# The second walk of a second feed-forward: its second product by 2x2 blocks, with weight operands kept in DRAM

## The chip, the cores and the metric

The kernel runs on one core of one Trainium2 chip. The metric is the device time of one execution in microseconds; the number quoted is the median of three runs. Besides the runs there is one profiled execution, whose page and trace are read here. TensorE multiplies matrices into the eight banks of PSUM; VectorE, ScalarE and GpSimd work elementwise, GpSimd on SBUF alone; SyncE (SP) issues all DMAs of this kernel, whose data go through 16 DMA engines. In the profile PE is TensorE, PEld its weight loads, DVE VectorE, ACT ScalarE, POOL GpSimd, SP SyncE.

## The reference, cut

```python
def _attn_ref(q, k, v):                    # 4 batches, 8 heads, 576 positions, 64 features
    scores = scale * np.matmul(q, k.transpose(0, 1, 3, 2))
    scores = np.where(block_i >= block_j, scores, -1e9)      # blocks of 64 positions
    attn = softmax(scores)
    return np.matmul(attn, v)

def _moe_ref(x, w_gate, w_val, w_out, rms_g):       # 2304 tokens, 512 -> 1536 -> 512
    xn = x / rms(x) * rms_g
    g = xn @ w_gate
    return (g * sigmoid(g) * (xn @ w_val)) @ w_out

def _moe2_ref(x, w_gate, w1, w2):                   # 8 experts, 512 -> 1024 -> 512
    logits = x @ w_gate
    P = np.exp(logits - logits.max())
    for _ in range(8):
        P /= P.sum(1, keepdims=True) + 1e-09
        P /= P.sum(0, keepdims=True) + 1e-09
        P *= N / E
    out = 0
    for e in range(E):
        h = np.maximum(x @ w1[e], 0.0)
        out += P[:, e:e + 1] * (h @ w2[e])
    return out
```

The function computes attention, then the first feed-forward on the 2304 x 512 result, then the second. In the second every token goes through all 8 experts, and P weighs what they return.

## The kernel before

**Precision.** Every large product is made from two-part operands: a value is split into a rounded high part (fp32r) and the rest, and a product is three matmuls, high by high, high by low and low by high (`THREE`). The helper `copy` makes the high part (line 294 on ScalarE, line 298 on VectorE), `minus` the low part (line 307, on GpSimd or VectorE). A split is thus one operation of each kind.

**Order.** Nothing is issued where it stands in the code. Each operation goes into `G` (class `Graph`) with an engine, a duration, what it reads and writes and, where two engines could do it, an alternative. A planner then lists all of them, forwards and backwards for twelve rounds, and the order with the earliest planned end is issued on each engine. Durations of type `Both` (two-input operations on GpSimd, and on VectorE where both inputs are in SBUF) exclude each other in the plan. SP's DMAs are ordered by the same plan. Buffers come from rings: the next use of a tile depends on all users of its last one.

**The second feed-forward, `moe2`.** Its input x stays in `acc[0]` to `acc[4]`, features on partitions, in token blocks of 512, 512, 512, 384 and 384 (`BL`). It is walked twice. `PASSES` (line 1028) names the token ranges of each walk: the first takes blocks 0 and 1 as one pair of halves of 512, the second blocks 3 and 4 as halves of 384 and block 2 as halves of 256. In each walk the loop runs over 8 experts and `NG` = 4 groups of two blocks of 128 hidden units; expert and group together are called a step here, 32 in a walk.

- `pass_operands` and `operands` prepare x for a walk: seven combinations of its 2x2 blocks, each split, into the tiles `xs` and, for a second pair of ranges, `more`. A combination of blocks is a subtraction (`add`, line 1064).
- `weights1` loads two raw blocks of w1 (`RAW`, 3 tiles), makes four sums of 256 columns (line 1064) and four split operand tiles (`W`, 9 tiles of [128, 2, 512]). Two w2 tiles come through `L.get` (line 330 for the DMA).
- `up` (line 1219) makes the first product by Strassen's seven products, six matmuls each, in three banks X, Y and Z of the four in `UP`. X takes products 0, 5, 6 and 3, and between them ScalarE keeps its sum (`keep`, line 1228); VectorE adds (`plus`, line 1233), ScalarE and VectorE apply relu and split the result into `HT2` (lines 1239, 1241).
- `down` (line 1275) makes the second product in the plain way: for each tile of 128 tokens, two hidden blocks by three terms, six matmuls of 512 columns into one of the three banks of `DN`. VectorE multiplies by P and adds into `acc`, over x (line 1290; for expert 0 lines 1281 and 1284). At the last step a tile goes to `out` (line 1294).
- `sink` computes P in the first step of the first walk, by a chain on VectorE with small matmuls (line 1177).

Both walks load w1 and w2 and prepare them again. `up` of a step stands ahead of `down` of the step before, and the planner mixes the two.

## Time and profile before

| | us |
|---|---|
| median of three runs | 2270.88 |
| lowest and highest run | 2269.70, 2271.71 |
| span of the profiled execution, first to last instruction | 2269.8 |
| TensorE busy in it | 2225.1 |
| VectorE, ScalarE, GpSimd busy | 1382.3, 986.1, 948.5 |

The profile gives no other time of the profiled execution than its span; it lies within the three runs. Attention and the first feed-forward take about the first 765 us, the first walk of the second feed-forward lasts to about 1415, the second to the end. Busy times are unions of the intervals of an engine's instructions; a matmul's own duration overlaps the next one's, so the time of one matmul is best read from the length of an unbroken row of them, divided by their count. The chain that ended last is followed back from the last instruction to what released it each time.

### The profile page before, as it was taken

The page shows a single profiled execution, that of the slowest core. Times are in us where ns is not written, and L with a number is a line of the kernel's source. Part 1 is how long each engine was busy: PE and PEld are TensorE (multiplying, and loading weights), DVE is VectorE, ACT ScalarE, POOL GpSimd, SP SyncE. Part 2 cuts the span into 40 slices and gives each one's busy share as a digit, 9 for nine tenths or more (in the row PEclk, how much of TensorE's full clock was granted, in tenths as well). Part 3 has the DMA queues.
Part 4 walks back from the last instruction along what each step waited for, and adds up shares of the span by engine and source line. Part 5 has one row for each costly group of instructions (what it writes and reads, how often), then busy time and mean ns, then how long its engine had stood idle before and what let it go on. Part 6 is the DMA issues. An engine that isn't in the chain of part 4 may idle for free.

```text
span 2269.8 us, 30396 instructions
## 1 busy us (share of the span) xinstructions
PE 2225.1 (98%) x11196; PEld 1908.5 (84%) x11196; DVE 1382.3 (61%) x2397; ACT 986.1 (43%) x2138; POOL 948.5 (42%) x899
## 2 busy tenths in 40 slices
PE   8799989999999999999999999999999999999999
PEld 6577778888999978888888888899999999999898
DVE  7879966776632566555555556655555555555555
ACT  6688756575311433333333334533333333333332
POOL 6555732321411544444444446543334443343431
PEclk8899999999999999999999999999999999999999
DMA  7645666443676111111111111211111111111111
GB/s 191 182 138 185 217 212 194 160 164 112 221 254 211 52 51 52 52 51 51 51 56 47 52 51 42 89 42 43 38 38 44 46 38 42 38 39 46 42 42 47
DMA packets 89416, 211.46 MB, mean 93 GB/s; under 512 B 14890, under 2 KB 18218, under 8 KB 89268
## 3 DMA queue, kind: packets, MB, share of 16 engines
q1 hardware_dynamic: 89268, 209.52, 29.7%
q8 instruction: 88, 1.44, 0.3%
q14 instruction: 60, 0.49, 0.1%
HBM read 185.89 MB, written 23.59 MB: 92 GB/s over the span
## 4 chain that ended last, share of the span: by engine, by line
PE 89%; DVE 7%; ACT 2%; issue 1%; POOL 1%; SPq 0%; DMA 0%; DVEq 0%; ACTq 0%; POOLq 0%
PE pm L1275 34%; PE ps L1219 24%; PE pm L913 11%; PE pm L1219 7%; PE pm L944 6%; PE ps L689 2%; PE ps L485 2%; PE po L732 1%; DVE mn L494 1%; PE po L1137 1%; DVE acc L354 1%; DVE acc L356 1%; PE po L599 1%; ACT p L679 0%; DVE ptl L696 0%
## 5 line engine op out<-in xcount | busy, mean ns | idle before, releaser
L1219 PE MATMUL ps<-xs,w 128*128 128x384 f32 (+2 forms) x2640 | 548.5, 350 | 0.0
L1290 DVE SCALAR_TENSOR_TENSOR acc<-pm,Pm,acc 128x512 f32<-128x512 f32 x504 | 378.1, 750 | 266.9 <-PE pm L1275 265.4
L1219 PEld LDWEIGHTS ps<-xs,w 128*128 128x128 f32 x2640 | 467.8, 189 | 51.6 <-issue 0.3
L1275 PE MATMUL pm<-w,h 128*128 128x512 f32 x1920 | 461.5, 390 | 0.0
L307 POOL TENSOR_TENSOR w<-raw,w 128x512 fp32r<-128x512 f32 (+1 forms) x289 | 345.2, 1204 | 173.8 <-ACT w L294 166.2
L1275 PEld LDWEIGHTS pm<-w,h 128*128 128x128 f32 x1920 | 354.1, 188 | 69.7
L307 POOL TENSOR_TENSOR w<-sp,w 128x512 fp32r<-128x512 f32 x126 | 170.0, 1350 | 511.4 <-ACT w L294 511.2
L1275 PE MATMUL pm<-w,x 128*128 128x512 f32 x1536 | 369.2, 391 | 0.0
L1275 PEld LDWEIGHTS pm<-w,x 128*128 128x128 f32 x1536 | 287.2, 188 | 56.9
L913 PE MATMUL pm<-x,w 128*128 128x512 f32 (+1 forms) x1440 | 331.0, 377 | 2.3 <-POOL w L307 1.4
L913 PEld LDWEIGHTS pm<-x,w 128*128 128x128 f32 x1440 | 259.5, 191 | 34.4 <-POOL w L307 2.2
L294 ACT ACTIVATE w<-sp 128x512 fp32r<-128x512 f32 x128 | 80.7, 631 | 292.4 <-PE pm L1275 286.9
L1228 ACT ACTIVATE ct<-ps 128x384 f32<-128x384 f32 (+2 forms) x152 | 75.9, 499 | 236.1 <-PE ps L1219 236.1
L1233 DVE TENSOR_TENSOR ct<-ps,ct 128x512 f32<-128x512 f32 (+2 forms) x154 | 86.2, 561 | 137.3 <-ACT ct L1228 71.3
L944 PE MATMUL pm<-h,w 128*128 128x512 f32 (+1 forms) x720 | 163.9, 374 | 1.2 <-DVE t L928 1.2
L294 ACT ACTIVATE w<-raw 128x512 fp32r<-128x512 f32 (+1 forms) x292 | 162.0, 575 | 6.2 <-PE pm L913 2.8
L1219 PE MATMUL pm<-xs,w 128*128 128x512 f32 (+2 forms) x720 | 155.6, 341 | 0.0
L307 POOL TENSOR_TENSOR h<-t,h 128x512 fp32r<-128x512 f32 (+1 forms) x56 | 67.7, 1209 | 195.8 <-ACT h L294 195.4
L944 PEld LDWEIGHTS pm<-h,w 128*128 128x128 f32 x720 | 129.6, 190 | 17.5 <-DVE t L928 1.6
L1219 PEld LDWEIGHTS pm<-xs,w 128*128 128x128 f32 x720 | 124.2, 188 | 17.4
L1239 ACT ACTIVATE h<-ct 128x384 fp32r<-128x384 f32 (+1 forms) x99 | 55.5, 561 | 89.5 <-DVE ct L1233 89.5
L1064 POOL TENSOR_TENSOR sp<-raw 128x256 f32<-128x256 f32 x64 | 51.5, 804 | 83.5 <-DMA raw<-w_dram 83.5
(268 smaller groups left out, 2892.0 us busy)
## 6 DMA issues: line engine op xcount, KB each, us to landing
raw<-w_dram SPq DMA_DIRECT2D x256, 256.0 KB, 2.6
w<-kg SPq DMA_DIRECT2D x48, 512.0 KB, 4.3
w<-kv SPq DMA_DIRECT2D x48, 512.0 KB, 3.9
w<-ko SPq DMA_DIRECT2D x48, 512.0 KB, 3.9
rq<-qT_dram SPq DMA_DIRECT2D x56, 144.0 KB, 4.2
rq<-kT_dram SPq DMA_DIRECT2D x52, 144.0 KB, 3.6
acc<-wg_dram SPq DMA_DIRECT2D x12, 512.0 KB, 4.2
acc<-wv_dram SPq DMA_DIRECT2D x12, 512.0 KB, 4.3
```

The costliest lines, as they stand in the source:

```text
L294: nc.scalar.activation(out=out_(), in_=in_(), func=AF.Copy, scale=scale)
L307: eng.tensor_tensor(out=out_(), in0=a(), in1=b(), op=ALU.subtract)
L485: nc.tensor.matmul(out=ps()[:, o : o + n], lhsT=a[:, 128 * t : 128 * t + 128], rhs=c[:, k0 : k0 + n], start=start, stop=stop)
L913: nc.tensor.matmul(out=ps()[:, 0:n], lhsT=w()[:, a, 128 * k : 128 * k + 128], rhs=xv()[:, c, k, 0:n], start=k == 0 and (a, c) == (0, 0), s ...
L944: nc.tensor.matmul(out=ps()[:, 0:n], lhsT=wos[q]()[:, a, 128 * m : 128 * m + 128], rhs=ht()[:, c, 0:n], start=q == 0 and (a, c) == (0, 0), ...
L1064: eng.tensor_tensor(out=out_(), in0=a(), in1=b(), op=op)
L1219: nc.tensor.matmul(out=bank()[:, 0:n], lhsT=w()[:, a, o + 128 * k : o + 128 * k + 128], rhs=views[p, q, i, k, c](), start=start and k == 0 ...
L1228: G.op("ACT", t_act(n, True), lambda: nc.scalar.activation(out=t()[:, 0:n], in_=bank()[:, 0:n], func=AF.Copy), r=[bank], w=[t])
L1233: G.op("DVE", t_v1(n), lambda: nc.vector.tensor_tensor(out=t()[:, 0:n], in0=bank()[:, 0:n], in1=t()[:, 0:n], op=ALU.add), r=[bank, t], w=[t])
L1239: G.op("ACT", t_act(n, psum), lambda: nc.scalar.activation(out=ht()[:, 0, 0:n], in_=src()[:, 0:n], func=AF.Relu), r=[src], w=[ht])
L1275: nc.tensor.matmul(out=y(), lhsT=hs[f][half]()[:, a, 128 * t : 128 * t + 128], rhs=ws[f]()[:, c, :], start=f == 0 and (a, c) == (0, 0), st ...
L1290: G.op("DVE", 63 + t_v1(512), lambda y=y, dst=dst, tt=tt, e=e: nc.vector.scalar_tensor_tensor(out=dst(), in0=y(), scalar=Pm()[:, tt, e : e ...
```

## The change

- The token ranges are dealt out anew. The first walk takes 1280 tokens in two groups, of width 384 (blocks 0 and 1) and 256 (the remaining 128 of each, against the first 256 of block 2, in two pieces). The second takes 1024 tokens in one group of width 512 (blocks 3 and 4, and the last 256 of block 2).
- In the first walk `down` is as before. Prepared w1 tiles are written to DRAM as they are (`keep_w`, `first_w`). `weights2` splits the two w2 tiles, makes four sums of them, splits these too into the ring `EX`, and writes what the second walk needs (`second_w`). The first walk's `CT` has 6 tiles in place of 7, and accumulators of block 2 lie in two pieces, so that x of the second walk stays.
- The second walk prepares no weights: `reload` reads seven tiles of 512 KB for the first product of two steps and seven for the second.
- In the second walk relu multiplies by P at once (`scaled`). P is turned in `sink`, written to DRAM and read back spread over the partitions, two DMAs for each half and expert (`load_p`).
- The second product works on a pair of steps, with the result's features on partitions: the two hidden blocks of a step, the two halves of the tokens and the two halves of the 512 features are its 2x2 blocks, and both steps of the pair are summed in the same banks. `sums` and `produce` make seven combinations of h's blocks, each split, in the ring `HL` (10 tiles, 14 used for a pair). `down2` makes seven products, each for two halves of 128 features and with six matmuls a half, in banks X, Y and Z, of which X again takes several products; after every product `gather` adds the bank to one of eight accumulators.
- At the end the accumulators are turned by 32 transposes, evicted, and stored.

The diff, its core:

```diff
-    PASSES = [[((0, 0), (1, 0), 512)], [((3, 0), (4, 0), 384), ((2, 0), (2, 256), 256)]]
+    PASSES = [[[((0, 0), (1, 0), 384)], [((0, 384), (2, 0), 128), ((1, 384), (2, 128), 128)]],
+              [[((3, 0), (4, 0), 384), ((2, 256), (2, 384), 128)]]]
+    WIDTH = [[sum(x[2] for x in q) for q in p] for p in PASSES]
+    LEFT = 10
...
+        def two(t, o, n):
+            return t[:, o : o + 2 * n].rearrange("p (a n) -> p a n", a=2)
+
+        HT2 = ring_of(order4 + [two(xt0, 768 * i, 384) for i in range(4)], [set(b.users) for b in HT[-4:]] + [done4] * 4)
+        pad = late(lambda p: p.tile([128, 4608], F32, name="pad"))
+
+        def cut(o, n):
+            return lambda: pad()[:, o : o + n]
+
+        atts = set(att_ops)
+        CT = ring_of([*T1.tiles, *(cut(3072 + 384 * i, 384) for i in range(4))],
+                     [set().union(*(b.users for b in T1[-2:]))] * 2 + [atts] * 4)
+        SP_ = ring_of([cut(512 * i, 512) for i in range(4)], [atts] * 4)
+        EX = ring_of([two(xt0, 3072, 512), lambda: two(pad().bitcast(F32R), 2048, 512)], [done4, atts])
...
+            pq = PO.next()
+            G.op("PE", 115, lambda: nc.tensor.transpose(
+                out=pq()[0 : (TT - LEFT) * E, 0:128], in_=Pm()[:, LEFT:TT, :].rearrange("p t e -> p (t e)"), identity=ident_t),
+                r=[Pm, ident], w=[pq])
+            G.op("ACT", 250, lambda: nc.scalar.activation(out=pt(), in_=pq()[0 : (TT - LEFT) * E, 0:128], func=AF.Copy), r=[pq], w=[pt])
+            G.op("SP", 300, lambda: nc.sync.dma_start(out=ptd_t.rearrange("t e n -> (t e) n"), in_=pt()), r=[pt], w=[ptd], lat=2000)
...
+        def keep_w(kept_, key, w, cols, g, prio):
+
+            if key not in kept_:
+                t = scr.tile([128, 2, 512], F32, name=f"{'f' if kept_ is first_w else 's'}{'_'.join(map(str, key))}")
+                kept_[key] = fixed(t, par=True)
+            b = kept_[key]
+            o = 0 if cols == 512 else 256 * (g % 2)
+            G.op("SP", 1900 * cols // 512, lambda: nc.sync.dma_start(out=b()[:, :, o : o + cols], in_=f32(w()[:, :, 0:cols])),
+                 r=[w], w=[b], prio=prio + 1, lat=2000)
...
+            for name, src, b, n in (("a", r0, [r0], 512), ("b", lambda: r1()[:, 256:512], [r1], 256), ("c", p0, s[0:2], 512), ("d", p1, s[2:4], 512)):
+                w = parts(src, b, n, W, prio)
+                keep_w(first_w, (name, e, g if n == 512 else g // 2), w, n, g, prio)
                 ws.append(w)
...
+        def weights2(e, g, prio):
+
+            r0, r1 = raws([w2[e, 128 * f : 128 * f + 128, :] for f in (GF * g, GF * g + 1)], prio)
+            ws = [parts(r_, [r_], 512, W, prio) for r_ in (r0, r1)]
+            p0, p1, s = sums4(lambda: r0()[:, 0:256], lambda: r1()[:, 0:256], lambda: r0()[:, 256:512], lambda: r1()[:, 256:512],
+                              (r0, r1, r0, r1), prio)
+            keep_w(second_w, ("a", e, g // 2), ws[0], 256, g, prio)
+            keep_w(second_w, ("b", e, g), ws[1], 512, g, prio)
+            for name, src, b in (("c", p0, s[0:2]), ("d", p1, s[2:4])):
+                keep_w(second_w, (name, e, g), parts(src, b, 512, EX, prio), 512, g, prio)
+            return ws
+
+        def reload(ring, kept_, order, prio):
+            out = {}
+            for key in order:
+                w, b = ring.next(), kept_[key]
+                G.op("SP", 1900, lambda w=w, b=b: nc.sync.dma_start(out=f32(w()), in_=b()), r=[b], w=[w], prio=prio, lat=2000)
+                out[key] = w
+            return out
...
-            h11 = relu(plus(Y, s1))
...
+        accc = [[Buf(place_c(j, t)) for t in range(k)] for j, k in ((0, 4), (1, 4), (2, 2))]
...
+        def second_pass():
+
+            N = WIDTH[1][0]
+            small = ended(CT, SP_, EX)
+            hops = ended(HT2, EX)
+            sides = ended(*more)
+            wbufs = W[-W.n :]
+            WL = ring_of([b.get() for b in wbufs] + [two(xt0, 1024 * i, 512) for i in (0, 1)], [set(b.users) for b in wbufs] + [hops] * 2)
+            HL = ring_of(order4 + [two(xt0, 1024 * i, 512) for i in (2, 3)] + [two(xt1, 1024 * i, 512) for i in range(4)],
+                         [hops] * 6 + [sides] * 4)
+            rb = RAW[-RAW.n :]
+            CF = ring_of([*T1.tiles, *(cut(512 * i, 512) for i in range(9)), rb[0].get()], [small] * 11 + [set(rb[0].users)])
+            xs = pass_operands(1, CF)[0]
+            used = ended(CF) | small | rb[0].users
+            over = [(j, i) for j, k in ((2, 4), (3, 3), (4, 3)) for i in range(k)]
+            CT1 = ring_of([*CF.tiles, *(acc[j][:, 512 * i : 512 * i + 512] for j, i in over)],
+                          [used] * CF.n + [read_x[j, 1] | ended(*accc[j : j + 1]) for j, i in over])
...
+            def scaled(src, half, n, psum=False):
+                t, P = CT1.next() if psum else src, pv_[0][half]
+                G.op("DVE", t_v1(n) if psum else t_vv(n), lambda: nc.vector.scalar_tensor_tensor(
+                    out=t()[:, 0:n], in0=src()[:, 0:n], scalar=0.0, in1=P(), op0=ALU.max, op1=ALU.mult),
+                    r=[src, P], w=[t])
+                return t
...
+            def diff(dst, x, y):
+                add(N, v(dst), v(x), v(y), op=ALU.subtract, r=[x, y], w=[dst], margin=GAIN)
+                return dst
+
+            def sums(h):
+                (b11, b12), (b21, b22) = h
+                got = {0: b11, 1: b21, 2: b22, 6: b12}
+                got[4] = diff(CT1.next(), b12, b11)
+                got[5] = diff(CT1.next(), b22, got[4])
+                return got
+
+            def produce(gots, ops, i):
+                ops[i] = []
+                for got in gots:
+                    if i == 6:
+                        diff(got[6], got[2], got[6])
+                    if i == 3:
+                        got[3] = diff(got[5], got[1], got[5])
+                    x, ht = got[i], HL.next()
+                    copy(G.op, N, lambda ht=ht: ht()[:, 0, 0:N], v(x), r=[x], w=[ht], margin=GAIN)
+                    minus(G.op, N, lambda ht=ht: ht()[:, 1, 0:N], v(x), lambda ht=ht: f32(ht()[:, 0, 0:N]), r=[x, ht], w=[ht], margin=GAIN)
+                    ops[i].append(ht)
...
+            def gather(bank, key):
+                dst = ac[key]
+                if key in begun:
+                    G.op("DVE", t_v1(N), lambda: nc.vector.tensor_tensor(out=dst(), in0=bank()[:, 0:N], in1=dst(), op=ALU.add),
+                         r=[bank, dst], w=[dst])
+                else:
+                    begun.add(key)
+                    G.op("ACT", t_act(N, True), lambda: nc.scalar.activation(out=dst(), in_=bank()[:, 0:N], func=AF.Copy), r=[bank], w=[dst])
...
+            def down2(e, grp, gots, ops):
+                g0, g1 = 2 * grp, 2 * grp + 1
+                ws = reload(WL, second_w, [("a", e, grp), ("b", e, g0), ("b", e, g1), ("c", e, g0), ("c", e, g1), ("d", e, g0), ("d", e, g1)], 0.5)
+                wts = {0: [(ws["a", e, grp], 256 * (g % 2)) for g in (g0, g1)]}
+                for i, name, o in ((1, "b", 0), (3, "b", 256), (4, "c", 0), (5, "c", 256), (6, "d", 0), (2, "d", 256)):
+                    wts[i] = [(ws[name, e, g], o) for g in (g0, g1)]
+
+                def m(i, dt, bank, start):
+                    def go():
+                        for gi in range(2):
+                            w, o = wts[i][gi]
+                            o += 128 * dt
+                            for a, c in THREE:
+                                nc.tensor.matmul(
+                                    out=bank()[:, 0:N], lhsT=w()[:, a, o : o + 128], rhs=ops[i][gi]()[:, c, 0:N],
+                                    start=start and gi == 0 and (a, c) == (0, 0), stop=gi == 1 and (a, c) == (1, 0),
+                                    skip_group_check=not start)
+
+                    G.op("PE", 6 * t_mm(N), go, r=[*(w for w, o in wts[i]), *ops[i]], w=[bank], prio=2.0)
+
+                X, Y, Z = {}, {}, {}
+                for i, B, new, key in ((0, X, True, (0, 0)), (1, Y, True, (0, 0)), (5, X, False, (0, 1)), (4, Z, True, (1, 1)),
+                                       (6, X, False, (1, 1)), (2, Z, False, (0, 1)), (3, X, False, (1, 0))):
+                    if i not in ops:
+                        produce(gots, ops, i)
+                    for dt in range(2):
+                        if new:
+                            B[dt] = (DX if B is X else DY).next()
+                        m(i, dt, B[dt], new)
+                        gather(B[dt], (*key, dt))
...
+            pend = None
+            for e in range(E):
+                load_p(e)
+                for grp in range(NG // 2):
+                    g0, g1 = 2 * grp, 2 * grp + 1
+                    f = reload(WL, first_w, [("a", e, g0), ("c", e, g0), ("d", e, g0), ("b", e, grp), ("a", e, g1), ("c", e, g1), ("d", e, g1)], 0.5)
+                    gots = []
+                    for g in (g0, g1):
+                        wa, wb, wc, wd = f["a", e, g], f["b", e, grp], f["c", e, g], f["d", e, g]
+                        gots.append(sums(up(1, 0, xs, [(wa, 0), (wa, 256), (wd, 256), (wb, 256 * (g % 2)), (wc, 0), (wc, 256), (wd, 0)], CT1, scaled)))
+                    if pend:
+                        down2(*pend)
+                    ops = {}
+                    for i in ORDER[:5]:
+                        produce(gots, ops, i)
+                    pend = (e, grp, gots, ops)
+            down2(*pend)
+            for half in range(2):
+                for t in range(N // 128):
+                    bank, stage = UP.next(), CT1.next()
+                    tt = LEFT + half_tiles[half][t]
+
+                    def turn(half=half, t=t, bank=bank):
+                        for m_ in range(4):
+                            nc.tensor.transpose(out=bank()[:, 128 * m_ : 128 * m_ + 128],
+                                                in_=ac[m_ // 2, half, m_ % 2]()[:, 128 * t : 128 * t + 128], identity=ident_t)
+
+                    G.op("PE", 4 * 115, turn, r=[ident, *(ac[d, half, dt] for d in range(2) for dt in range(2))], w=[bank], prio=2.0)
+                    G.op("ACT", t_act(512, True), lambda bank=bank, stage=stage: nc.scalar.activation(out=stage(), in_=bank(), func=AF.Copy),
+                         r=[bank], w=[stage],
+                         alts=[("DVE", t_v1(512), lambda bank=bank, stage=stage: nc.vector.tensor_copy(out=stage(), in_=bank()))])
+                    G.op("SP", 1100, lambda stage=stage, tt=tt: nc.sync.dma_start(out=out[128 * tt : 128 * tt + 128, :], in_=stage()), r=[stage])
+
+        first_pass()
+        second_pass()
```

## Rows read from the trace of the kernel before

**Rows 1.** the page: span, busy time by engine, GB/s in 40 slices

```profile
span 2269.8 us, 30396 instructions
...
PE 2225.1 (98%) x11196; PEld 1908.5 (84%) x11196; DVE 1382.3 (61%) x2397; ACT 986.1 (43%) x2138; POOL 948.5 (42%) x899
...
GB/s 191 182 138 185 217 212 194 160 164 112 221 254 211 52 51 52 52 51 51 51 56 47 52 51 42 89 42 43 38 38 44 46 38 42 38 39 46 42 42 47
```

**Rows 2.** the windows by stage; the first line names the columns

```profile
core 0: us, PE busy (x) PEld busy (x) DVE busy (x) ACT busy (x) POOL busy (x), PEclk, DMA share, GB/s
...
1500.00:2250.00 750.00, 750.00 (x4142) 678.83 (x4141) 409.95 (x700) 258.60 (x570) 284.15 (x281) 1.00 0.14 39
620.00:670.00 50.00, 50.00 (x290) 50.00 (x290) 17.86 (x33) 8.14 (x16) 8.10 (x8) 1.00 0.76 254
780.00:820.00 40.00, 38.11 (x174) 30.98 (x173) 33.38 (x79) 19.56 (x35) 20.71 (x19) 1.00 0.16 48
1400.00:1440.00 40.00, 40.00 (x194) 34.36 (x194) 34.60 (x49) 20.05 (x46) 28.54 (x30) 1.00 0.23 76
```

**Rows 3.** the chain that ended last, first walk: start us, us, what

```profile
850.12 4.08 PE ps L1219 x18
...
919.92 8.18 PE pm L1275 x36
932.23 4.08 PE ps L1219 x18
```

**Rows 4.** the same chain, second walk, two steps apart

```profile
1530.52 4.18 PE ps L1219 x24
...
1582.70 5.22 PE ps L1219 x30
```

**Rows 5.** groups by shape, 800 to 2270 us: count | busy us, mean ns | idle

```profile
L307 POOL TENSOR_TENSOR w<-raw,w 128x512 fp32r<-128x512 f32 x181 | 237.0, 1324 | 124.6 <-ACT w L294 124.0 <-DMA raw<-w_dram 0.6
...
L294 ACT ACTIVATE w<-raw 128x512 fp32r<-128x512 f32 x183 | 108.3, 623 | 0.0
...
L1064 POOL TENSOR_TENSOR sp<-raw,raw 128x256 f32<-128x256 f32 x61 | 46.7, 765 | 0.0
...
L1284 DVE TENSOR_TENSOR acc<-pm,acc 128x512 f32<-128x512 f32 x54 | 37.3, 691 | 29.8 <-PE pm L1275 29.3
...
L1228 ACT ACTIVATE ct<-ps 128x512 f32<-128x512 f32 x49 | 29.3, 598 | 52.8 <-PE ps L1219 52.7
```

**Rows 6.** timeline of GpSimd in the first walk: start us, us, engine, line

```profile
1010.95 1.29 POOL L307 TENSOR_TENSOR w<-sp,w 128x512 fp32r<-128x512 f32 x1 [4.20 <-ACT w L294]
...
1017.75 1.47 POOL L307 TENSOR_TENSOR w<-raw,w 128x512 fp32r<-128x512 f32 x1
```

**Rows 7.** timeline of VectorE there

```profile
999.95 1.01 DVE L1241 SCALAR_TENSOR_TENSOR x<-t,x 128x512 fp32r<-128x512 f32 x1
...
1005.47 0.68 DVE L1241 SCALAR_TENSOR_TENSOR x<-t,x 128x512 fp32r<-128x512 f32 x1
```

**Rows 8.** DMA issues: KB each, median us from issue to landing

```profile
w<-kg SPq DMA_DIRECT2D x48, 512.0 KB, 4.3
...
kg<-w SPq DMA_DIRECT2D x12, 512.0 KB, 4.3
```

**Rows 9.** groups by shape, TensorE, whole span: the transposes of attention

```profile
L689 PE MATMUL ps<-ident,p 128*128 128x128 f32 x247 | 54.5, 292 | 3.2 <-ACT p L679 1.8 <-ACT p L501 1.3
```

**Rows 10.** the end of the chain, 2240 to 2270 us

```profile
2266.09 0.75 DVE acc L1290
```

**Rows 11.** tile xs, 1395 to 1480 us: count, ns min/median/max, first and last start

```profile
L307 DVE TENSOR_TENSOR xs<-ct,xs x7: 545/959/1368, 1410.0 to 1432.6; 128x384 fp32r<-128x384 f32 x6, 128x256 fp32r<-128x256 f32 x1
...
L307 POOL TENSOR_TENSOR xs<-acc,xs x3: 1013/1057/1193, 1403.6 to 1419.2; 128x384 fp32r<-128x384 f32 x2, 128x256 fp32r<-128x256 f32 x1
```

**Rows 12.** the chain between the walks

```profile
1412.56 8.18 PE pm L1275 x36
```

**Rows 13.** timeline of TensorE early in the first walk; idle before it in brackets

```profile
798.71 0.39 PE L1177 MATMUL po<-sm,onec 128*128 128x8 f32 x2 [1.18 <-DVE sm L1165]
```

269 lines of the change are left out of this document (163 added, 106 removed).

## The prediction

> **What bounds the kernel now.** I read the page first: TensorE is busy for 98% of a span of 2269.8 us [rows 1]. The windows by stage come next, because a mean over attention, first feed-forward and second feed-forward says little about one of them. In the second walk of the second feed-forward (1500 to 2250 us) TensorE is busy for 750.00 of 750 us, VectorE for 410, ScalarE for 259, GpSimd for 284; the granted clock is 1.00, the upper level of 2.4 GHz, and the DMA engines move 39 GB/s [rows 2]. The chain of waits through both walks holds matmuls and nothing else. In the first walk the same place of the pattern returns after 82.11 us, which is four steps of 20.53 us; in the second walk two steps take 52.18 us, or 26.09 each [rows 3, 4]. So this part is worth what its matmuls cost: a matmul taken away is time taken away, as long as the other engines and the transfers stay under it.
>
> One 512-column matmul costs 8.18 / 36 = 0.2272 us [rows 3]. The Trainium skill (TensorE: Matmul & The Clock Gate, "Back-to-back issue gap") gives about 0.2157 us for a warm one; the row is 5% above that, the row decides, and by the page's figure the saving below would be 41.4 us in place of 43.6.
>
> **The matmuls.** A step is one expert and two blocks of 128 hidden units; there are 32 in a walk. Before, the first walk takes 1024 tokens and the second 1280. The change swaps this: the first now takes 1280 in widths 384 and 256 (the old second walk's shapes), the second 1024 in width 512 (the old first walk's). The first product is already Strassen's and keeps its counts at each width, so it costs the same. The second product was (8 + 10) token tiles x 6 matmuls x 32 steps = 3456 of 512 columns. After: 10 x 6 x 32 = 1920 in the first walk, and in the second 16 pairs of steps with 7 products x 2 halves x 2 steps x 3 terms = 84 each, so 1344. That is 192 fewer: 192 x 0.2272 = **-43.6 us**. A pair of steps of the second walk holds 84 + 84 matmuls, 168 x 0.2272 = 38.2 us; a step of the first should stay at 26.1.
>
> **The tail.** The new accumulator has features on partitions, so 8 tiles are turned at the end by 32 transposes of 128x128. The attention's are the nearest row, 54.5 / 247 = 0.22 us each [rows 9]: **+7.0 us**, all after the last product, since nothing else is left for TensorE. Bounds: 3.5 if the half whose sums end first is turned under the last product, 9 if its banks wait for their copies. What follows, one eviction and one store, replaces the 0.75 us addition and the store that end the old chain [rows 10]; I count that as nothing.
>
> **The first walk's added work.** Per step w2 gets four 256-column sums and two more operand pairs, on GpSimd 4 x 0.765 + 2 x 1.324 = 5.7 us, on ScalarE 2 x 0.62 = 1.2 us [rows 5]. The old second walk has 284/750 x 26.09 = 9.9 us of GpSimd and 9.0 of ScalarE in a step [rows 2]; 15.6 and 10.2 stay under 26.1, so the price is nothing. It costs if GpSimd work is late, and the slack against that is 10 us a step. Eight stores join four loads on SP's queue: 3.67 MB out, 1.05 MB in, 181 GB/s. The loads of the next raw weights stand behind those stores on SP; a 512 KB store lands in a median of 4.3 us, a load the same [rows 8], and 254 GB/s have been moved at 620 to 670 us under a TensorE that never paused [rows 2]. Price nothing, with the second rival for the case that this is wrong.
>
> **The second walk's moved work.** The raw loads, sums and splits of the weights go; they were hidden, so nothing is gained. Seven 512 KB loads per product come instead: 14 x 0.524 MB in 38.2 us, 192 GB/s, under the 254 shown [rows 2]. The tiles are asked for half a pair (19 us) or at least half an up-product pair (9.5 us) ahead of use, against 4.3 us to land [rows 8]. New is the work on h: per pair of steps 8 differences and 14 subtractions on GpSimd or VectorE, 14 copies on ScalarE or VectorE, 14 gatherings from PSUM and 14 operations that end the first product on VectorE. At the rows' durations: GpSimd 22 x 1.29 = 28.4 us if it takes all [rows 6]; VectorE 22 from PSUM x 0.691 + 6 from SBUF x 0.68 = 19.3 us [rows 5, 7]; ScalarE 6 x 0.598 + 14 x 0.623 = 12.3 us [rows 5]. All lie under 38.2. The gathering that a bank waits for has three products of other banks, 3 x 1.36 = 4.1 us, to be done in. I take 0.15 us a pair for waits, +2.4 us; bounds 0 and 1.0 a pair.
>
> What speaks against this is that GpSimd and VectorE don't run freely beside each other. VectorE's two-SBUF-input operation takes 0.68 us alone and 1.01 beside GpSimd [rows 7], GpSimd's 1.29 and 1.47 [rows 6]. The Trainium skill (SBUF — State Buffer, "Who interferes with whom") says why: such an operation and one of GpSimd hold the shared pair one at a time, each for a whole instruction. By that rule the two columns add, and the trace's stretched rows agree.
>
> Added, GpSimd's 28.4 and VectorE's six, 4.1, make 32.5 us of 38.2: 85%, still under. Each operation moved from GpSimd to VectorE takes 0.6 us off. With all at their stretched lengths it is 22 x 1.47 + 6 x 1.01 = 38.4, just at TensorE's 38.2. That is the first rival.
>
> **The two transitions.** Into the first walk: TensorE idles 1.9 us in 780 to 820, part of it in the chain of normalising steps (one wait of 1.18 us on VectorE) [rows 2, 13]. The operands now come in three pieces of 384, 128 and 128 columns, three times the instructions for 640 columns in place of 512, and VectorE is busy 33 of 40 us there. I add 1.5, bounds -1.9 and 8. Between the walks: before, all is hidden (40.00 of 40 us busy) [rows 2], since after the last up-product at 1412.56 two full second products are left to do [rows 12]. Now 10 tiles are left, 10 x 1.36 = 13.6 us, and up to four products that need no kept sum, 5.4 us, together 19. Preparing the operands is 44 two-input operations, half of 384 and half of 128 columns. A 384 one takes 0.96 us on VectorE in the median and 0.55 at best, 1.06 on GpSimd [rows 11]; with both engines at it about 0.5 each, and 0.25 for the short ones, 22 x 0.75 = 16.5 us, and VectorE also drains ten banks. The first kept sum waits for the whole preparation, because its ring begins with the same buffers. So it ends 18 to 22 us after the last up-product: 0 to 3 us idle. Then two pairs of up-products run with no second product to fill the time in which a bank is read, some 0.7 us (0.598 [rows 5] and a hand-over) once in each of four. Together **+4 us**, bounds 0 and 10.
>
> **The sum**, on the profiled span: 2269.8 - 43.6 + 7.0 + 2.4 + 1.5 + 4 = 2241.1. The runs' median, 2270.88, is 1.1 above that span: **2242 us**.
>
> **Rivals.** *The shared pair decides the second walk.* The sum at stretched lengths, 38.4 of 38.2, says it is close; a gathering queued behind a blocked VectorE operation then lets a bank wait. Against it: the stretched row is the exception, and the planner treats the pair as exclusive when it orders the work. Price: one GpSimd operation's wait, 1.29 us, per pair, 16 x 1.29 = 21 us: 2263. Chance 0.17.
>
> *The transfers decide (the slower one).* Stores of the first walk at 141 GB/s have no row: before, the whole trace has 36 weight stores, three groups of 12 [rows 8]. If the mix of stores and loads falls below 4.72 MB in 26.98 us, 175 GB/s, each step loses the 0.89 us that is its share of the 28.6 us gained, and the kernel is no faster. At 160 GB/s a step takes 29.5 us: 32 x 3.4 = 109 us, 2351. For it: the slices of the span in which those stores fall moved between 112 and 217 GB/s, though nothing says that they wanted more [rows 1]; against it: 254 under loads [rows 2]. Chance 0.06.
>
> *The up-products aren't filled.* The second walk has two up-products of a step pair in a row. If the order doesn't put second products between them, each loses about 0.7 us where its bank is read, 32 x 0.7 = 22 us: 2264. The old first walk mixes them, and the new one has as many fillers as products. Chance 0.09.
>
> *The change does less than it says*, the saved matmuls given back by an idle TensorE in unforeseen places: 2271. Chance 0.04.
>
> **How the numbers follow.** The forecast has the remaining 0.64. Its own bounds: 2242 less 3.5 (tail), 2.4, 3.4 and 4 is 2229 if all fall together; plus 2, 14, 6.5 and 6 is 2270, as unlikely. The range 2232 to 2264 leaves out the slower cases and the extremes. A measurement of this kernel tells 0.2% from nothing: below 2266.3 all of the forecast but 0.01, and the first and third rival nearly whole, 0.87; between, 0.05; above 2275.4, 0.08.
>
> **What would show it.** After: 11196 - 192 + 33 = 11037 matmuls; first-walk steps of 26.1 us at some 180 GB/s; pairs of 38.2 us in the second walk, VectorE and GpSimd both under 0.9 there; GpSimd busy near 15.6 of 26.1 in a first-walk step; a gap of a few us between the walks; some 7 us more between the last product and the end. A pair of 39.5 us with TensorE waiting for VectorE points to the first rival, a step well over 26 us with waits on DMA to the second, gaps behind ScalarE's evictions to the third. The forecast is wrong if any steady step is not TensorE's.

## The result and the profile after

The changed kernel takes 2245.28 us (median of 4 runs, 2244.82 to 2247.61) against 2270.29 of the kernel before beside it: a ratio of 0.9892, with a 95% interval from 0.9878 to 0.9906. It is faster by 1.1%, 25 us where 29 were forecast. The profiled execution has a span of 2243.6 us, 26.2 less than before.

The page of the changed kernel, the lines that answer to [rows 1]:

```profile
span 2243.6 us, 31476 instructions
...
PE 2196.7 (98%) x11037; PEld 1884.6 (84%) x11037; DVE 1445.1 (64%) x2450; ACT 990.3 (44%) x2140; POOL 1167.4 (52%) x1077
...
HBM read 273.97 MB, written 141.07 MB: 185 GB/s over the span
```

The count of matmuls is the one forecast, 11037, and TensorE's busy time falls by 28.4 us. GpSimd works 219 us more. The windows of the changed kernel by stage (columns: us, then busy time and instructions of each engine, granted clock, DMA share, GB/s), beside [rows 2]: three in which the routing is computed, the first walk, the place between the walks, the second walk.

```profile
755.00:765.00 10.00, 10.00 (x50) 10.00 (x50) 4.30 (x9) 2.90 (x7) 5.82 (x6) 0.66 0.57 211
765.00:775.00 10.00, 10.00 (x43) 10.00 (x43) 3.90 (x8) 2.84 (x10) 4.01 (x8) 0.51 0.08 26
775.00:785.00 10.00, 6.65 (x33) 6.02 (x32) 7.89 (x20) 3.35 (x11) 7.43 (x13) 0.84 0.13 52
830.00:1600.00 770.00, 770.00 (x4256) 697.07 (x4255) 437.59 (x729) 300.64 (x652) 445.96 (x454) 1.00 0.51 179
1600.00:1640.00 40.00, 38.52 (x177) 31.18 (x176) 28.85 (x49) 16.77 (x41) 22.72 (x27) 1.00 0.75 261
1740.00:2180.00 440.00, 439.99 (x1921) 359.44 (x1920) 300.95 (x384) 142.59 (x233) 257.05 (x192) 1.00 0.60 198
```

Both walks are still TensorE's, to the last hundredth in the first and 439.99 of 440 in the second, at the upper clock. In the second walk VectorE is busy for 68% and GpSimd for 58%. What stands out is the start: TensorE counts as busy from 755 to 775 us, at a mean of 0.66 and then 0.51 of its clock, which is in the second of these windows nearly all the time the lower level of 1.2 GHz; then it is idle for a third of 775 to 785.

The chain of waits (start us, us, what) in the first walk, two steps apart, and in the second, at the same place of the pattern three pairs of steps apart; it answers to [rows 3, 4]:

```profile
932.99 5.22 PE ps L1296 x30
...
985.14 5.22 PE ps L1296 x30
...
1739.57 4.08 PE pm L1518 x18
...
1855.33 4.08 PE pm L1518 x18
```

A step of the first walk takes 52.15 / 2 = 26.08 us (26.1 forecast), a pair of the second 115.76 / 3 = 38.59 (38.2, and 0.15 for waits). A part of the 0.4 us above the matmuls is in the walks of before too, whose step of 20.53 us holds 90 matmuls, 90 x 0.2272 = 20.45; the table counts what is added.

Where the 26.2 us come from, by comparing TensorE's start-to-start times in the two traces, stage by stage (the matmuls' row is their count at the row's rate; 0.2 us are not placed):

| | forecast | measured |
|---|---|---|
| 192 matmuls less | -43.6 | -43.6 |
| attention and first feed-forward (same order of matmuls in both) | 0 | -1.6 |
| start of the first walk, with the routing | +1.5 | +8.5 |
| steady first walk | 0 | 0 |
| between the walks | +4 | +2.6 |
| waits in the second walk | +2.4 | +3.6 |
| tail | +7.0 | +4.5 |
| sum | -28.7 | -26.0 |

### The profile page after: what moved, and what is told of

Its sections match the earlier page's. It is cut to its first block, busy times and chain, and to the rows that moved or that the text cites. A ratio compares the mean times of both kernels' runs of the same rounds, so it can differ in the third digit from the quotient of the medians.

```text
span 2243.6 us, 31476 instructions
## 1 busy us (share of the span) xinstructions
PE 2196.7 (98%) x11037; PEld 1884.6 (84%) x11037; DVE 1445.1 (64%) x2450; ACT 990.3 (44%) x2140; POOL 1167.4 (52%) x1077
## 4 chain that ended last, share of the span: by engine, by line
PE 89%; DVE 7%; ACT 2%; issue 1%; POOL 1%; DMA 0%; SPq 0%; DVEq 0%; ACTq 0%; POOLq 0%
PE ps L1296 23%; PE pm L1361 19%; PE pm L913 11%; PE pm L1518 11%; PE pm L1296 7%; PE pm L944 6%; PE po L1518 3%; PE ps L689 2%; PE ps L485 2%; PE po L732 1%; PE po L1157 1%; DVE mn L494 1%; DVE acc L354 0%; PE po L599 0%; DVE acc L356 0%
## 5 line engine op out<-in xcount | busy, mean ns | idle before, releaser
L1376 DVE SCALAR_TENSOR_TENSOR acc<-pm,Pm,acc 128x512 f32<-128x512 f32 x280 | 209.9, 750 | 158.5 <-PE pm L1361 155.5
L1361 PE MATMUL pm<-w,h 128*128 128x512 f32 x1152 | 279.7, 391 | 0.0
L307 POOL TENSOR_TENSOR w<-raw,w 128x512 fp32r<-128x512 f32 (+1 forms) x157 | 190.5, 1223 | 117.2 <-ACT w L294 109.4
L1361 PEld LDWEIGHTS pm<-w,h 128*128 128x128 f32 x1152 | 209.9, 188 | 39.3
L1361 PE MATMUL pm<-w,x 128*128 128x512 f32 x768 | 187.4, 392 | 0.0
L1361 PEld LDWEIGHTS pm<-w,x 128*128 128x128 f32 x768 | 143.0, 188 | 26.8
L1499 DVE TENSOR_TENSOR acc<-pm,acc 128x512 f32<-128x512 f32 x169 | 116.7, 690 | 74.4 <-PE pm L1518 73.2
L1296 PE MATMUL pm<-xs,w 128*128 128x256 f32 (+2 forms) x654 | 138.9, 336 | 0.0
L1310 DVE TENSOR_TENSOR pad<-ps,pad 128x384 f32<-128x384 f32 (+2 forms) x127 | 66.2, 521 | 107.1 <-ACT pad L1305 64.1
L307 POOL TENSOR_TENSOR x<-pad,x 128x512 fp32r<-128x512 f32 (+1 forms) x75 | 96.4, 1287 | 69.3 <-ACT x L294 69.1
L1518 PE MATMUL pm<-x,w 128*128 128x512 f32 x510 | 126.4, 391 | 0.5 <-DVE x L307 0.5
```

The source lines that it names most:

```text
L307: eng.tensor_tensor(out=out_(), in0=a(), in1=b(), op=ALU.subtract)
L1296: nc.tensor.matmul(out=bank()[:, 0:n], lhsT=w()[:, a, o + 128 * k : o + 128 * k + 128], rhs=views[p, q, i, k, c](), start=start and k == 0 ...
L1310: G.op("DVE", t_v1(n), lambda: nc.vector.tensor_tensor(out=t()[:, 0:n], in0=bank()[:, 0:n], in1=t()[:, 0:n], op=ALU.add), r=[bank, t], w=[t])
L1361: nc.tensor.matmul(out=y(), lhsT=hs[f][half]()[:, a, o : o + 128], rhs=ws[f]()[:, c, :], start=f == 0 and (a, c) == (0, 0), stop=f == GF - ...
L1376: G.op("DVE", 63 + t_v1(512), lambda y=y, dst=dst, tt=tt, e=e: nc.vector.scalar_tensor_tensor(out=dst(), in0=wide(y()), scalar=Pm()[:, tt, ...
L1499: G.op("DVE", t_v1(N), lambda: nc.vector.tensor_tensor(out=dst(), in0=bank()[:, 0:N], in1=dst(), op=ALU.add), r=[bank, dst], w=[dst])
```

## The experiments

### The kept operands alone

The kernel before, in which the first walk stores both products' operands and the second loads them; the second product stays plain.

```
+            if p:
+                wa, wb, wc, wd = (load_w((x, e, g), prio) for x in "abcd")
...
-                ws.append(w)
+                ws.append(store_w((name, e, g), w, n, prio))
```

> The kernel before with one part of the change: the first walk writes both products' weight operands to DRAM and the second walk reads them back; token ranges and the plain second product stay. If the gain comes from the 192 matmuls alone, the weights' preparation was hidden and its removal is worth nothing: 2270 us, within 2 us of the kernel before, second-walk steps still 26.1 us, GpSimd's busy time in the second walk near 0. If the preparation of the weights had held the second walk back somewhere, 2250 to 2262. If the added transfers cost something, first-walk steps over 20.6 us (3.9 MB in 20.5 us, 190 GB/s) and a time over 2275.

Measured 2271.31 us, ratio 0.9999 (0.9990 to 1.0009). The window of its second walk:

```profile
1500.00:2240.00 740.00, 740.00 (x4083) 669.26 (x4083) 398.03 (x691) 173.54 (x397) 0.00 (x0) 1.00 0.33 109
```

GpSimd falls from 284 us in 750 [rows 2] to nothing, and no time is won: the preparation of the weights had been hidden whole. What the change gains is the second product's. That the kept operands are needed to make room for its work on h is not tested by itself; the run below with 18 us more of such work in each pair, which lost much, speaks for it.

### The same saving once more

The last and best version below (2237.07) with 192 matmuls less again: of products 1 and 2 only the first inner block is multiplied, so the output differs.

```
+                    half_ = 1 if i in (1, 2) else 2
...
-                        for gi in range(2):
+                        for gi in range(half_):
```

> The version with dense logits, own users and the later gather (2237.07) with as many matmuls again taken out of the second walk as the change took out: of two of its seven products (1 and 2) only the first of the two inner blocks is multiplied, 12 matmuls of 512 columns less in each of 16 pairs of products, 192 in all, so that the output is not the reference's; operands, gathers and transfers stay. Theory, that TensorE sets the second walk alone and each matmul is worth its 0.2272 us: a pair goes from 38.4 to 35.7 us and the whole to 2193 to 2197 (43.6 us less, up to 3 of them lost to new waits). Rival, that VectorE and GpSimd stand close behind: by the run with three low parts made twice (2258.6, 13 us more for 7.8 us of work a pair) a work that takes 59% of the two engines at 38.4 us takes 63% at 35.7 and 73% in that run, so some loss begins between; with a loss of 5 to 13 us the whole comes at 2199 to 2207.

Measured 2203.1 us (2202.95 to 2203.31): 34.0 less, not 43.6. By the total the rival holds, but the trace puts the loss elsewhere. TensorE's timeline (start us, us, line, count), first product and last transposes, of the version without and with the cut:

```profile
1648.61 1.52 PE L1528 MATMUL pm<-h,w 128*128 128x512 f32 x6
...
2231.76 0.60 PE L1570 MATMUL pm<-ident,acc 128*128 128x128 f32 x4
```

```profile
1656.15 1.52 PE L1530 MATMUL pm<-h,w 128*128 128x512 f32 x6
...
2195.47 0.60 PE L1572 MATMUL pm<-ident,acc 128*128 128x128 f32 x4
```

That stretch goes from 583.15 to 539.32 us: 43.8 less, all of it. TensorE doesn't pause in the steady part, with VectorE busy for 75% and GpSimd for 62% of it:

```profile
1740.00:2120.00 380.00, 380.00 (x1667) 312.63 (x1666) 283.28 (x363) 128.81 (x213) 235.50 (x171) 1.00 0.65 216
```

But the stretch begins 7.5 us later, 6.5 of them already at the end of attention, which the cut doesn't touch. Its order does differ: the planner orders the whole kernel anew for each edit. From 20 to 110 us the granted clock is 0.83 with the cut and 0.88 without. So a matmul of the second walk is worth its 0.2272 us, and no second bound lies within the 2.7 us that a pair became shorter; and a total of one program against another carries some us of the order that was planned.

### The shared pair, tested

The prediction's first rival. Low parts in the second walk are made twice, the second time with the same values: in all seven products, then in three.

```
-                    minus(G.op, N, lambda ht=ht: ht()[:, 1, 0:N], ...
+                    for _ in range(2):
+                        minus(G.op, N, lambda ht=ht: ht()[:, 1, 0:N], ...
```

> The changed kernel with every low-part subtraction of the second walk's operands made twice (the second writes the same values): about 14 more operations of 1.3 us in each pair of products, 18 us of work on the pair VectorE/GpSimd. In the changed kernel a pair of products takes 38.6 us, in which VectorE works 26 us (68%) and GpSimd 23 us (58%), together 49 of 77. My theory is that this pair of engines has room and TensorE alone sets the 38.6 us: then 67 of 77 us are taken, GpSimd rises to 85 to 95%, the pair of products stays below 39.3 us and the whole is within +12 us of 2245 (2243 to 2257). The rival of the prediction, that the pair of engines decides in the second walk: the waits grow with the work, a pair of products takes 41 us or more (half of 18 us is shown as 2.4 us or more), the whole 2285 or later.

Measured 2362.99 us, ratio 1.0401: my theory of ample room falls. The window from 1740 to 2180 us:

```profile
1740.00:2180.00 440.00, 386.30 (x1619) 307.67 (x1617) 367.96 (x438) 113.66 (x192) 277.88 (x185) 0.96 0.50 169
```

TensorE now idles 54 of 440 us, though GpSimd is busy for only 63% and VectorE for 84% of the time. The timeline of VectorE shows how the room is lost:

```profile
1959.54 0.69 DVE L1500 TENSOR_TENSOR acc<-pm,acc 128x512 f32<-128x512 f32 x1
1960.14 1.73 DVE L307 TENSOR_TENSOR x<-pad,x 128x512 fp32r<-128x512 f32 x1
1961.80 1.78 DVE L307 TENSOR_TENSOR h<-t,h 128x512 fp32r<-128x512 f32 x1
1963.49 1.78 DVE L307 TENSOR_TENSOR x<-pad,x 128x512 fp32r<-128x512 f32 x1
1965.20 1.78 DVE L1079 TENSOR_TENSOR t<-acc,t 128x512 f32<-128x512 f32 x1
1966.90 1.76 DVE L1444 SCALAR_TENSOR_TENSOR acc<-acc,raw 128x512 f32<-128x512 f32 x1
1968.59 0.68 DVE L1310 TENSOR_TENSOR acc<-ps,acc 128x512 f32<-128x512 f32 x1
```

An operation with two SBUF inputs takes 1.73 to 1.78 us there where it takes 0.68 alone [rows 7], and the sum that TensorE waits for (L1310) stands behind five of them. A reading from PSUM is not stretched, 0.69. This is what the Trainium skill says (SBUF — State Buffer, "Who interferes with whom"): one of the two holds the pair for a whole instruction; the trace agrees, GpSimd's operations beside these five taking up to 1.75 us for 1.29 [rows 6]. The idle shares of the two engines, each read by itself, overstate the room, since what one does in its idle time stretches the other.

> The changed kernel with the low-part subtraction made twice in three of the seven products of the second walk (all seven: 2363, 7.4 us a pair of products for 14 more operations). Here 6 more operations, 7.8 us of work a pair. Theory 1, that there is room and then a point from which the pair VectorE/GpSimd decides: all of 7.8 us still fits into the room, a pair of products stays within 0.6 us of 38.6, the whole within 10 us of 2245. Theory 2, that there is no room and each added operation costs from the first on (0.4 us for each us added, as in the run with all seven): 3.1 us a pair, the whole 2290 to 2300.

Measured 2258.59 us (2250.54 to 2260.68), ratio 0.9942 (0.9922 to 0.9963). Between the two theories, nearer the first: 13 us, or 0.8 a pair, for 7.8 us of work a pair. In the profiled run VectorE is busy for 75% and GpSimd for 71% of that window, and the second walk takes 12 us more than the changed kernel's beyond its matmuls. These aren't spread evenly: 11.8 us are ten waits, 6.3 of them for VectorE, 2.6 for ScalarE, 2.9 for loads. So the rival's point lies between 14 added operations, which cost 7.4 us a pair, and none; with six the waits have begun. The changed kernel stands just below it: a small wait in its pairs, shown further below, is of this kind.

### The transfers, tested

The second rival. The first walk stores its operands a second time to a place that nobody reads: all, then half of them (the second run's edit; `HALF` is "ad", and the first run has no such condition).

```
+            if key[0] in HALF:
+                G.op("SP", 1900 * cols // 512, lambda: nc.sync.dma_start(out=t2, in_=f32(w()[:, :, 0:cols])), ...
```

> The changed kernel in which the first walk writes every weight operand to DRAM twice, the second copy to a place that nobody reads: 3.7 MB more in each step of 26.08 us, so that the first walk asks for 320 GB/s in place of 179. My theory, that transfers do not set the first walk and have room beyond what the change asks: steps stay at 26.1 us and the whole within 4 us of 2245 (2241 to 2250). The rival of the prediction, that the transfers become the bound not far above the rate of the kernel before: with a limit near 200 GB/s a step would take 8.3 MB / 200 GB/s = 42 us, the whole some 500 us later; with a limit near 280 GB/s 29.8 us a step and some 75 to 120 us later.

Measured 2415.69 us, ratio 1.0635: 170 us more, 5.3 a step, which neither limit that I named gives. The window 850 to 1250 us, then what the engines waited for in it (us in total, times, longest us), then the same for the queue that issues the transfers:

```profile
850.00:1250.00 400.00, 372.04 (x1955) 333.13 (x1953) 214.06 (x335) 131.66 (x287) 198.73 (x199) 0.96 0.70 259
```

```profile
PE ps L1302 <- POOL w L307: 19.3, 7, 2.9
...
ACT w L294 <- DMA again<-w: 33.4, 14, 3.7
```

```profile
SPq L1251 <- POOL w L307: 177.4, 40, 9.6
```

It moves 259 GB/s. The weight buffers wait for the second copy to land (ACT on "again"), their operands come late, TensorE waits for those; and the queue that issues the stores stands still behind one that isn't ready.

> The changed kernel in which the first walk writes half of its weight operands to DRAM a second time (the copies of a and d of both products): 1.84 MB more in each step of 26.08 us, so that the first walk asks for 250 GB/s in place of 179. Written twice in full (320 asked) the run moved 259 GB/s, 5.3 us a step more. Theory, that the limit lies where that run stood, near 260 GB/s: 250 still passes, the whole within 12 us of 2245. Rival, that the second copy costs by what it holds up (the buffers that it reads and the queue in which it stands) and not by a limit of the rate: about half of the full run's loss, 2.6 us a step, the whole 2310 to 2340.

Measured 2240.6 us (2237.26 to 2244.96), ratio 0.9871: no loss. Its window:

```profile
850.00:1250.00 400.00, 400.00 (x2208) 362.10 (x2207) 247.97 (x389) 155.75 (x336) 229.55 (x232) 1.00 0.70 254
```

254 GB/s, stores and loads mixed, under a TensorE that never pauses. So the rival's 175 GB/s was far off; the changed kernel's 179 leaves some 75 GB/s. Whether the full copy met a limit of the rate near 260 or only its own buffers and queue, these two runs don't tell apart.

### The start of the first walk

This was the largest miss, 8.5 us for 1.5. TensorE's timeline in the changed kernel; idle time before a group in brackets:

```profile
762.72 2.92 PE L1157 MATMUL po<-gwr,acc 128*128 128x8 f32 x24
765.49 2.27 PE L1296 MATMUL ps<-xs,w 128*128 128x384 f32 x6
767.55 5.12 PE L1157 MATMUL po<-gwr,acc 128*128 128x8 f32 x24
772.53 2.27 PE L1296 MATMUL ps<-xs,w 128*128 128x384 f32 x6
...
781.89 0.39 PE L1199 MATMUL po<-sm,onec 128*128 128x8 f32 x2 [3.35 <-DVE sm L1187]
```

Six 384-column matmuls take 2.1 us from start to start at 765 and at 772, and 1.05 in a steady step: half the clock. Both groups stand behind blocks of routing logits, matmuls that stream 8 columns each. At 781.89 TensorE waits 3.35 us for the normalising chain on VectorE, where the kernel before waited 1.18 [rows 13]. What each of the two is worth shows in the window of the whole start, before and after:

```profile
700.00:830.00 130.00, 128.11 (x671) 116.13 (x670) 67.41 (x137) 42.64 (x82) 52.14 (x47) 0.93 0.29 93
700.00:830.00 130.00, 126.05 (x693) 120.61 (x692) 68.86 (x149) 44.64 (x102) 64.96 (x74) 0.88 0.48 170
```

TensorE is idle for 2.1 us more, not far from the 1.5 forecast, and the granted clock is lower by 0.05, which over 130 us is some 6.5 us of full clock. The two together come to the 8.5. The second is an estimate: clock that is lost where TensorE would wait anyway costs nothing.

In the first test of the clock the logits are turned round: 8 weight columns stay, 512 or 384 token columns stream, and 18 small transposes follow (1.6 us). TensorE needs as long for it (40 matmuls in 15.9 us, for 144 in 16.0 at full clock). In the second, three quarters of the logits' products are left out, so the output differs.

```
-                        nc.tensor.matmul(out=ps()[:, E * t : E * t + E], lhsT=raw_x(j, 128 * t, k, 128), rhs=gwr()[:, k, :], ...
+                    nc.tensor.matmul(out=ps()[0:E, 0:n], lhsT=gwr()[:, k, :], rhs=raw_x(j, 0, k, n), ...
```

> The changed kernel, with the router's logits made the other way round: 8 weight columns stay in TensorE and 512 or 384 token columns stream, then 18 small transposes, in place of 72 products that stream 8 columns each. The start of the first walk lost 8.5 us against the kernel before where 1.5 were forecast. Theory A: the granted clock fell to half in long stretches behind the blocks of 8-column products, and the products after them ran at 1.2 GHz. Then the clock stays up, 384-column products at 765 to 785 us take 174 ns and not 320, and the time falls by 5 to 9 us, to 2237 to 2240. Theory B: the wait for the normalising chain on VectorE and the operands in three pieces set the start: 2244 to 2247, with TensorE idle in place of slow.

> The changed kernel with three quarters of the router's logit products left out (only the first 128 of 512 features count, so P and the output differ). 108 short products less, about 12 us at 0.111 us each. Theory A (clock): the blocks are a quarter as long, the clock stays at its upper level between 710 and 790 us, and the gain is 12 + 5 to 9, so 2224 to 2228. Theory B (the chain on VectorE sets the start): TensorE waits longer for the chain, the gain is under 12, 2233 to 2240.

Measured 2239.69 us (2239.11 to 2240.6), 5.6 less than the changed kernel, and 2226.05, 19.2 less, where 12 are the work left out. From 700 to 830 us the granted clock is 0.99 and 0.97 in these two. The dense version's windows:

```profile
755.00:765.00 10.00, 10.00 (x47) 6.31 (x45) 7.24 (x11) 3.15 (x8) 7.18 (x9) 1.00 0.59 210
765.00:775.00 10.00, 6.44 (x33) 5.39 (x32) 7.05 (x22) 6.08 (x20) 8.37 (x17) 0.90 0.24 95
775.00:785.00 10.00, 9.64 (x61) 8.70 (x60) 9.45 (x28) 4.85 (x13) 4.58 (x6) 0.93 0.30 106
```

The clock stays up through the logits for the same work; it falls once, behind a wait of 3.19 us on VectorE that ends at 772.81. A part of what the clock gives turns into idle time. Is this the change's, or any kernel's? The same in the kernel before:

> The kernel before with the logits computed the dense way (8 weight columns stationary, 512 or 384 token columns streaming, then small transposes), as in the run of the changed kernel with dense logits (2239.7). Theory A, that the half clock behind the 8-column logits is a matter of either kernel and of chance from execution to execution, not of this change: the kernel before gains 4 to 7 us as the changed one did, 2264 to 2267, with a smaller spread, and the change is worth 25 to 28 us between the two dense kernels. Theory B, that the change itself made the start slower: the kernel before gains 2 us or less (2269 to 2271), and the change is worth 30 us or more between the two.

Measured 2271.12 us, ratio 0.9997 (0.9988 to 1.0006): nothing won, though the granted clock from 700 to 830 us rises from 0.93 to 0.97, so theory A falls by its numbers and theory B's come out. A count helps: from 560 to 900 us, the time that TensorE doesn't spend on large matmuls at full clock is 30.6 us before and 31.3 with dense logits, but 39.3 after and 32.2 with dense logits. With the dense ones the starts are 0.9 us apart, near the forecast's 1.5, and the change is worth 2271.12 - 2239.69 = 31.4 us; the other terms of the table and 0.9, without the -1.6 of stages that the change doesn't touch, give -32.0. So the extra is gone where the clock stays up. That the clock alone brings it is not shown, since the plan also begins the dense logits earlier (at 674 us in the changed kernel, the others at 711). But why here?

> The kernel before with only the token ranges of its walks altered: the first walk takes the pieces of 384 and 256 columns (the changed kernel's first walk has 384 and 2 x 128), the second 384 and 128; the plain second product and the weights' preparation in both walks stay, and the number of columns that TensorE streams is the same. The dense logits brought the changed kernel 5.6 us and the kernel before nothing, so the slow start belongs to the change and not to chance alone. From 560 to 900 us TensorE spends 30.6 us on other than the large matmuls at full clock in the kernel before (25.6 in a run with the same start), 34.5 to 39.3 in the four runs with the start of the changed kernel. Theory: the narrower ranges are the cause (a group of six up-products between two blocks of logits lasts 1.05 us at 384 columns in place of 1.36 at 512, and fewer products are there to fill the waits for the routing): 34 to 39 us in that window here too, and the whole 2275 to 2280. Rival: the operands' copies to DRAM and the order that is planned around them are the cause: 25 to 31 us, and the whole 2268 to 2273.

Measured 30.2 us in that window (31.6, less 1.4 of attention that had slipped into it): the narrower ranges aren't the cause, that theory falls too. Its second walk reads its last 256 tokens from tiles that the first walk has overwritten, so the values differ, not the work. The whole took 2365.23 us, 95 more, mostly because pieces of 128 columns are dear, as the last section shows.

The rival of that run, the stores and the order around them, is not shown either: in the run with the stores written half again, whose start has the changed kernel's work, the window cost 30.9 us, in those with other stores or second walks 33.0 to 38.2, in the kernel with kept operands 25.6. So the slow start doesn't come with the change as such, and theory B doesn't hold either. And each trace is one execution: the version with own users below took 2237.14 us at a mean granted clock of 0.986, and 2243.84 to 2246.88 at 0.981 to 0.984. So the size varies by 8 us among programs whose start has the same work, and by several us among executions of one. Why one order, or one execution, falls to the lower clock for longer than another stays open.

### Between the walks, and a wait in each pair

The changed kernel's timeline between the walks and at a place of the second walk that returns in most pairs, then VectorE at that place:

```profile
1622.45 1.33 PE L1296 MATMUL ps<-xs,w 128*128 128x512 f32 x3 [1.24 <-ACT xs L294]
1623.93 1.66 PE L1296 MATMUL ps<-xs,w 128*128 128x512 f32 x6 [0.15 <-ACT t L1305]
...
1744.84 2.88 PE L1518 MATMUL pm<-x,w 128*128 128x512 f32 x12
1747.73 0.93 PE L1518 MATMUL pm<-h,x 128*128 128x512 f32 x3
```

```profile
1745.65 1.33 DVE L307 TENSOR_TENSOR h<-acc,h 128x512 fp32r<-128x512 f32 x1
1746.90 0.68 DVE L1499 TENSOR_TENSOR acc<-pm,acc 128x512 f32<-128x512 f32 x1
```

The twelve matmuls at 1744.84 and the three behind them take 0.25 us more than 0.227 each. The second bank's product ends the row of twelve; the product at 1747.73 goes into the first one's, whose gathering starts only at 1746.90, behind a subtraction that took 1.33 us where 0.68 is its length alone [rows 7], and ends at 1747.58. The wait stands in ten of the walk's pairs, each time behind a subtraction of 1.27 to 1.33 us: some 10 x 0.24 = 2.4 of the 3.6 us in the table. So this wait is the prediction's first rival, the gathering queued behind a stretched operation, on a small scale.

In the first experiment on these, the second walk's first buffers wait for their own last users in place of all. In the second, with the dense logits besides, 450 ns are planned between a product and the gathering of its bank.

```
-            used = ended(CF) | small | rb[0].users
+            gone = [small] * 11 + [set(rb[0].users)]
...
+                          [set().union(gone[k], *(b.users for b in CF[k :: CF.n])) for k in range(CF.n)] + ...
...
-                    G.op("PE", 6 * t_mm(N), go, r=[...], w=[bank], prio=2.0)
+                    G.op("PE", 6 * t_mm(N), go, r=[...], w=[bank], prio=2.0, lat=450)
```

> The changed kernel, in which a kept sum of the second walk's first up-product waits for the last users of its own buffer only, no longer for all operands of the walk. Between the walks TensorE waited 1.24 us for a split on ScalarE and lost 2.6 us in all. If the wait for the whole preparation is the cause, 1 to 2.5 us of it go: 2243 to 2244. If the preparation itself is what comes last (the operand that the product needs), nothing changes: 2245, the same 2.6 us.

> The changed kernel with the dense logits, with the first buffers of the second walk's sums waiting for their own last users only, and with 450 ns more between a product of the second walk and the gathering of its bank in the order that is planned, so that two products rather than one stand between a bank's gathering and its next use. Theory: the 0.27 us a pair that TensorE waits for the gathering of product 3's bank goes away, 16 x 0.27 = 4.3 us, and about 1 us between the walks: 2234 to 2236. Rival, that the wait has another cause (the order of products is bound by the buffers of the operands): it stays or moves to another product, 2238 to 2240.

The first: 2244.93 us (2237.14 to 2246.88), not to be told from the changed kernel's, whose start varies by more; in the trace the loss between the walks falls from 2.6 to 1.5 us, as expected. The second: 2237.07 us (2236.03 to 2238.4), ratio 0.9846 (0.9833 to 0.9860), the best of all. From 1740 to 2140 us what TensorE spends over its matmuls falls from 4.0 to 1.8 us, and the wait in each pair is gone. The whole is 2.6 us less than the dense version and not 4 to 5, since the wait stood in ten pairs and not in sixteen. The run with half the stores doubled, whose second walk is the changed kernel's, has it in two pairs only: so how much stands between a gathering and the next use of its bank belongs to the order that was planned, and the 450 ns are one way to another order.

## Why the prediction was right, and where its terms were off

**The bound and the matmuls held.** The views said that both walks are TensorE's; both still are, and 192 x 0.2272 = 43.6 us came out whole. The cut of another 192 gave 43.8 in the second walk. The rate of 0.2272 from the row held, against the shorter gap that the Trainium skill gives (TensorE: Matmul & The Clock Gate, "Back-to-back issue gap").

**The first walk's added work was hidden**, as forecast: GpSimd 445.96 / 770 x 26.08 = 15.1 us a step (15.6 forecast), 179 GB/s (181), step 26.08. The slack named is real: half the stores again cost nothing. **The second walk's moved work** was hidden too, but for the wait shown above and by a smaller margin than the sum suggested. GpSimd takes 257.05 / 440 x 38.59 = 22.5 us of a pair and VectorE 26.4. The groups by shape, 1740 to 2180 us (count | busy, mean ns | idle before):

```profile
L307 POOL TENSOR_TENSOR x<-acc,x 128x512 fp32r<-128x512 f32 x40 | 54.8, 1376 | 17.7 <-ACT x L294 17.4
...
L1444 DVE SCALAR_TENSOR_TENSOR acc<-acc,raw 128x512 f32<-128x512 f32 x30 | 28.6, 954 | 0.7
...
L1499 DVE TENSOR_TENSOR acc<-pm,acc 128x512 f32<-128x512 f32 x129 | 89.1, 690 | 55.4 <-PE pm L1518 54.4
```

The prediction took the stretched lengths as the exception; in the mean they are the rule (954 ns for 0.68 alone). The gatherings read PSUM and keep their 0.69, but they can start late behind a stretched operation. The rival was real and near: a wait of 0.25 us in most pairs is of its kind already, and with a quarter more of such work it costs some 0.8 more. Its price, one wait of 1.29 us a pair, was of the right size.

**The start was mis-sized**, 8.5 for 1.5. The waits that I had in mind came to 2.1; the sum had no term for the clock, to which the rest is put down. That the bounds (-1.9 and 8) were nearly right was luck: I looked for waits on VectorE, where the row of before shows idle time, and not at the granted clock, which falls in the kernel before as well. Its window, behind a block of logits:

```profile
730.00:740.00 10.00, 10.00 (x53) 10.00 (x52) 1.11 (x2) 0.69 (x2) 0.00 (x0) 0.66 0.36 121
```

A busy TensorE at the lower clock doesn't show as idle time.

**The tail** cost 4.5 us for 7.0. Timeline of the end:

```profile
2233.78 1.47 PE L1560 MATMUL ps<-ident,acc 128*128 128x128 f32 x12
2235.01 1.64 PE L1518 MATMUL po<-h,w 128*128 128x512 f32 x6
...
2237.44 1.42 PE L1560 MATMUL ps<-ident,acc 128*128 128x128 f32 x11 [0.24 <-DVE acc L1499]
2238.69 0.60 PE L1560 MATMUL pm<-ident,acc 128*128 128x128 f32 x4
```

From start to start a transpose takes (2235.01 - 2233.78) / 12 = 0.103 us and (2238.69 - 2237.44) / 11 = 0.114, half of the 0.22 that I took from attention's busy time [rows 9]; there they stand mostly in groups of one to five, between smaller ones, and the end of each group counts with it. So 32 are some 3.5 us. That 12 go ahead of the last product, as for the lower bound, saves nothing by itself: TensorE spends their time there in place of later. The remaining 1.0 us is what follows the last product, which I had counted as nothing. **Between the walks** 2.6 of 4, in the place named. **The waits of the second walk** 3.6 of 2.4: the size is near, its reason failed. I had three products of other banks, 4.1 us, in which to gather; in the planned order one stood there, 1.36 us, and a stretched subtraction of 1.33 us ahead of the gathering is then enough for a wait.

The two sums of the table are 2.7 us apart: +7.0 at the start against -2.7 in the other terms, and -1.6 in stages that the change doesn't touch.

## What to carry to other kernels

Where a stage shows TensorE busy to the last hundredth at full clock, a matmul less is a time less, at the rate of the chain of waits, and the work that pays for it is free until it delays what the matmuls wait for. Take the granted clock as a second column beside busy time: what stands behind matmuls that stream few columns can cost twice its length with no idle time to show for it. A planner that orders the whole kernel anew moves untouched stages by some us with each edit, so compare a change stage by stage, not by totals alone.

## What the runs showed of the hardware

- Width of a matmul: 0.2270 us for 512 columns, 0.174 for 384, 0.120 for 256, 0.111 for 128, from start to start. Below 256 columns hardly anything more is won. The kernel with narrow pieces shows it on the timeline of TensorE, groups of three 0.33 to 0.34 us apart, where in the changed kernel 256 columns take 0.36:

```profile
1815.07 0.50 PE L1219 MATMUL pm<-x,w 128*128 128x128 f32 x3
1815.40 0.50 PE L1219 MATMUL ps<-xs,w 128*128 128x128 f32 x3
```

  512 columns cut to 384 and 128 cost 0.058 us more, 1344 times: 78 of its 95 us.
- The granted clock fell to 0.51 over 10 us in which TensorE counted as busy, around blocks of 8-column matmuls; with the same products streaming 512 or 384 columns it stayed at 0.90 or more in each of the 10 us windows shown.
- Stores and loads together moved 254 GB/s for 400 us without a pause of TensorE.
